# Decayed linear attention feeding a SwiGLU block: the second token tile enters by pairs of batches, and the last ramp evacuation moves to VectorE

## The chip, the cores and the metric

The kernel runs on one core of a Trainium2 chip. The metric is the device time of one execution in microseconds (us), the median of several runs. The engines are named as in the profile: PE is TensorE (matrix multiplication; PEld its weight loads), DVE is VectorE, ACT is ScalarE, POOL is GpSimd and SP is SyncE, which here only issues transfers.

## What is computed

Four batches, eight heads, 768 positions, 64 channels a head. Attention is linear with a decay per head, worked in blocks, with a state carried from block to block; its output, 3072 tokens by 512, goes through a SwiGLU block with 1536 inner features.

```python
for b in range(nb):                                   # blocks of positions
    intra = einsum('bhic,bhjc->bhij', qb, kb) * Dmask # lam**(i-j) below the diagonal
    intra = einsum('bhij,bhjd->bhid', intra, vb)
    inter = einsum('bhid,bhde->bhie', qb * lam_pow, kv_state)
    out[:, :, sl] = intra + inter
    kv_state = lam_block * kv_state + einsum('bhsd,bhse->bhde', kb * rev_pow, vb)
x = out.transpose(0, 2, 1, 3).reshape(B * S, H * D)
g = x @ w_gate
y = (g / (1 + exp(-g)) * (x @ w_val)) @ w_out
```

Inputs and output are float32; the kernel multiplies in bfloat16 and sums in float32.

## The kernel before

**Tiles.** The positions are cut into six tiles of 128 (`NBLK = 6`). A tile holds these 128 positions of all four batches, so 512 tokens. For each tile attention makes `xt`, the transposed input of the SwiGLU block (128 x 4 x 512, bfloat16), and the SwiGLU block then runs in 12 units, one for each 128 inner features, followed by output products for each batch.

**A unit** is `ffn_fc` (L404), made of `ffn_gv` and `ffn_h`: four matmuls of 512 columns into `gp` (L390), SiLU on ACT into `sil` (L392), four matmuls into `vp` (L395), and the product `h_sb` on DVE (L402). **An output** is `ffn_out` (L408): twelve matmuls over the inner features (L415), a copy `osb` on ACT (L418), and a transfer to memory on SP's queue (L419). Tile 0's outputs are made in two halves of 256 columns each, because `w_out` is loaded in two halves: the first half of columns after tile 0's units, the second half among tile 1's units.

**Attention pieces.** In tiles 0 and 1 the score matrix of a whole 128-position block is made. `prep_k` and `prep_q` (L227, L234) transpose k and q of one batch on PE, with the evacuation on ACT for k (L232) and on DVE for q (L238). `front0` (L263) makes the scores of a batch (L271) and DVE multiplies them by the decay mask into `ssb` (L275). `values0` (L280) multiplies by v (L291), in tile 1 also adds the state's part (L289), and `evac` (L277) brings the sum from PSUM to `xt` on ACT (L278). `scale_k` (L294) scales k on ACT for the state, one head at a time. `update0` (L309) multiplies the scaled k by v into `up` (L315) and decays the state in float32 on DVE (`kvd`, L321; in tile 1 first the sum, L319). `cast_kv` (L323) puts the state into bfloat16 on ACT (L326, L307).
From tile 2 on, a tile is handled in two halves of 64 positions, in two groups `p` of two batches: `turn` (L240) transposes k and q by a transfer on SP's queue; `scale_q` (L245, DVE L248) and `move_q` (L252, eight transfers on SP's queue) place the scaled q in `zbuf`; `front` (L356) makes the scores in the one buffer `spb` (L362); `masks` (L364) writes them to `zbuf` on DVE (L367, two instructions a group); `update` (L330) makes the state's sums (L338), `update_mid` (L341) the state in the middle of the tile on DVE (L343), `cast_mid` (L345) its copy in `ybuf` on ACT (L307, two a group); `values` (L369) multiplies (L377) and evacuates with `evac`.

**Order.** The program's order is written out by hand and is the order on each engine. A list of units is run through for each tile `tt` (L511 to L544), and after unit number i the attention pieces registered for i are run: `add(first, i, ...)` for those run during tile 0's units (they prepare tile 1), `add(second, i, ...)` for those during tile 1's (they finish tile 1's state and prepare tile 2). Each engine works strictly through its own list, waiting on semaphores.

**Ramp.** Before the first unit PE works through tile 0's attention (L422 to L444). `idle(n)` multiplies zeros n times, to keep PE at work while it waits; `values0(0, (b,), n)` does so n times ahead of the values of batch b, and `ffn_gv` twice ahead of the first unit.

**Loads.** POOL's queue takes them in this order after the ramp's: gate and value weights in seven slices of columns (`load_w`, L447), two clearings of `kvb` on POOL itself, q and k of tile 1 (whole tiles), the first half of `w_out` (`load_wo(0)`), v of tile 1 in two halves, k and q of tile 2. During tile 1 `hold(2)` (L259), a tiny copy on POOL that needs tile 2's transposed q, keeps the rest of POOL's queue back: the second half of `w_out`, tile 2's v, all of tile 3.

**PSUM.** Of eight banks, two are `spb` and six serve the pool `psum`, from which `gp`, `vp`, `up`, `op`, `tk`, `tq`, `sp` and `ffn_op` are taken.

Of the kernel before, what the change touches and what calls it, by code (L numbers as in the profile page):

```python
# [8 lines left out]
FP32 = mybir.dt.float32  # L9
BF16 = mybir.dt.bfloat16  # L10
U32 = mybir.dt.uint32
AF = mybir.ActivationFunctionType
ALU = mybir.AluOpType
# [8 lines left out]
def kernel(  # L22
# [16 lines left out]
    nc = tc.nc  # L39

    B, H, S, D = q.shape
    HP = H // 2
    BLK = 128
# [3 lines left out]
    MC = DM // 128  # L47
    FC = DFF // 128
    TT = B * BLK
# [9 lines left out]
    opool = ctx.enter_context(tc.tile_pool(name="opool", bufs=3))  # L59

    spsum = ctx.enter_context(tc.tile_pool(name="spsum", bufs=1, space=bass.MemoryType.PSUM))
    psum = ctx.enter_context(tc.tile_pool(name="psum", bufs=6, space=bass.MemoryType.PSUM))
# [21 lines left out]
    def load_nat(t, tt, b0=0, b1=B):  # L84

        d, name = (qn, "q_nat") if t is q else (kn, "k_nat") if t is k else (vn, "v_nat")
        if tt not in d:
            d[tt] = load.tile([128, B * H, D], BF16, name=name, tag=name)
        nc.gpsimd.dma_start(out=d[tt][:, b0 * H:b1 * H], in_=blk_ap(t, tt, b0, b1))  # L89
# [102 lines left out]
    wg_sb = const.tile([128, MC, DFF], BF16, name="wg_sb")  # L192
# [3 lines left out]
    def load_w(f0, f1):  # L196
        for t, w in ((wg_sb, moe_w_gate), (wv_sb, moe_w_val)):
            nc.gpsimd.dma_start(out=t[:, :, f0:f1], in_=w.rearrange("(c p) f -> p c f", p=128)[:, :, f0:f1])  # L198
# [15 lines left out]
    def xt_of(tt):  # L214
        if tt not in xts:
            xts[tt] = xpool.tile([128, MC, TT], BF16, name="xt", tag="xt")
        return xts[tt]
# [56 lines left out]
        for h in range(2):  # L274
            nc.vector.tensor_tensor(out=ssbs[tt, b][:, h], in0=sp[h], in1=mask0[:, h], op=ALU.mult)  # L275

    def evac(tt, b, op):  # L277
        nc.scalar.copy(out=xt_of(tt)[:, :, b * BLK:(b + 1) * BLK], in_=op)  # L278

    def values0(tt, bs, wait=0):  # L280

        for b in bs:
            op = psum.tile([128, HP, 128], FP32, name="op", tag="b")
            idle(wait, op.rearrange("p n t -> p (n t)"))
            ssb = ssbs.pop((tt, b))
            for hp in range(HP):
                i = b * HP + hp
                for h, ps in enumerate(HALVES if tt else ()):
                    nc.tensor.matmul(op[ps, hp, :], kvb[:, i, h, :], qts[tt][:, i, :], start=True, stop=False)  # L289
                for h, ps in enumerate(HALVES):  # L290
                    nc.tensor.matmul(op[ps, hp, :], vn[tt][:, 2 * i + h, :], ssb[:, h, hp, :], start=(tt == 0), stop=True)  # L291
            evac(tt, b, op)

    def scale_k(tt, h):  # L294

# [5 lines left out]
    def fp32_kv(name):  # L301
        return att.tile([128, NPP, D], FP32, name=name, tag=name)
# [6 lines left out]
    def update0(tt, p):  # L309

        up = psum.tile([128, NPP, D], FP32, name="up", tag="b")
        for n in range(NPP):
            for h, ps in enumerate(HALVES):
                i = 2 * (p * NPP + n) + h
                nc.tensor.matmul(up[ps, n, :], ks[tt][:, i, :], vn[tt][:, i, :], start=True, stop=True)  # L315
        kvn[p] = up
        if tt:
            kvn[p] = fp32_kv("kv32")
            nc.vector.tensor_tensor(out=kvn[p], in0=kvd[p], in1=up, op=ALU.add)  # L319
        kvd[p] = fp32_kv("kvd")  # L320
        nc.vector.tensor_tensor(out=kvd[p], in0=kvn[p], in1=lam64 if tt else lam128, op=ALU.mult)  # L321

# [58 lines left out]

    hs, gv = {}, {}

    def ffn_gv(tt, fc, wait=0):
        xt = xt_of(tt)
        fs = slice(fc * 128, (fc + 1) * 128)
        gp = psum.tile([128, TT], FP32, name="gp", tag="b")
        idle(wait, gp)
        for mc in range(MC):
            nc.tensor.matmul(gp, wg_sb[:, mc, fs], xt[:, mc, :], start=(mc == 0), stop=(mc == MC - 1))  # L390
        sil = opool.tile([128, TT], BF16, name="sil", tag="sil")
        nc.scalar.activation(sil, gp, AF.Silu)  # L392
        vp = psum.tile([128, TT], FP32, name="vp", tag="b")
        for mc in range(MC):
            nc.tensor.matmul(vp, wv_sb[:, mc, fs], xt[:, mc, :], start=(mc == 0), stop=(mc == MC - 1))  # L395
        gv[tt, fc] = sil, vp

    def ffn_h(tt, fc):
        sil, vp = gv.pop((tt, fc))
        if tt not in hs:  # L400
            hs[tt] = hpool.tile([128, FC, TT], BF16, name="h_sb", tag="h")
        nc.vector.tensor_tensor(out=hs[tt][:, fc, :], in0=sil, in1=vp, op=ALU.mult)  # L402

    def ffn_fc(tt, fc):  # L404
        ffn_gv(tt, fc, 2 if tt == fc == 0 else 0)
        ffn_h(tt, fc)

    def ffn_out(tt, b, i=0, parts=1):  # L408

# [31 lines left out]
    values0(0, (0,), 2)  # L441
    front0(0, 3)
    for b in range(1, B):
        values0(0, (b,), b)  # L444


    for f0, f1 in ((0, 128), (128, 256), (256, 512), (512, 768), (768, 1024), (1024, 1280), (1280, 1536)):  # L447
        load_w(f0, f1)
    for h, ps in enumerate(HALVES):
        nc.gpsimd.memset(kvb[ps, :, 1 - h].bitcast(U32), 0)  # L450
    load_nat(q, 1)
    load_nat(k, 1)
    load_wo(0)
    for b in (0, 2):
        load_nat(v, 1, b, b + 2)
    load_nat(k, 2)
    load_nat(q, 2)

# [1 line left out]
    def add(at, i, *piece):  # L460
        at.setdefault(i, []).append(piece)

    def attention(tt, at, sq, su, sf, sv):

        for p in range(2):
            add(at, sq[p], scale_q, tt, p)
            add(at, sq[p], move_q, tt, p)
            add(at, su[p], update, tt, p, range(1 if tt in (2, NBLK - 1) else 2))
        for p in range(2):
            add(at, sf[p], front, tt, p)  # L470
            add(at, su[p], update_mid, p)
            if 2 < tt < NBLK - 1:
                add(at, su[p], update_end, p)
                add(at, su[p] + 2, cast_kv, tt + 1, p)
            add(at, su[p] + 1, cast_mid, tt, p)
            add(at, sf[p], masks, tt, p)
        for b in range(B):
            add(at, sv, values, tt, b)

    first = {}  # L480
    for h in range(H):
        add(first, h // 2, scale_k, 0, h)
    for i in range(4):
        add(first, 5 + i, half_constants, i // 2, i % 2)
    for p in range(2):
        add(first, 4, update0, 0, p)
        add(first, 5 + p, cast_kv, 1, p)
    for b in range(B):
        add(first, 9 + b // 2, prep_q, 1, b)
        add(first, 11, prep_k, 1, b)  # L490
    for b in range(B):
        add(first, 11 + b // 2 + b // 3, front0, 1, b)
    for p in range(2):
        add(first, 14, values0, 1, range(2 * p, 2 * p + 2))
    add(first, 14, turn, 2, k)
    add(first, 14, turn, 2, q)
    second = {}
    add(second, 0, hold, 2)
    add(second, 0, load_wo, 1)
    add(second, 0, load_v, 2)  # L500
    add(second, 0, load_tile, 3)
    for h in range(H):
        add(second, h // 3, scale_k, 1, h)
    for h in range(H):
        add(second, (4, 4, 5, 5, 8, 8, 9, 9)[h], scale_k, 2, h)
    for p in range(2):
        add(second, 4, update0, 1, p)
        add(second, 6 + p, cast_kv, 2, p)
    attention(2, second, (5, 6), (11, 11), (6, 9), 14)

    for tt in range(NBLK):  # L511
        units = [(ffn_fc, tt, fc) for fc in range(FC)]
        if tt == 0:
            units += [(ffn_out, 0, b, 0, 2) for b in range(B)]
        elif tt == 1:
            outs = [(ffn_out, 0, b, 1, 2) for b in range(B)]
            units = units[0:10] + outs[0:1] + units[10:11] + outs[1:2] + units[11:12] + outs[2:4]
        else:
            units = sum([units[3 * b:3 * b + 3] + [(ffn_out, tt - 1, b)] for b in range(B)], [])
        pieces = {}  # L520
        if tt < 2:
            pieces = (first, second)[tt]
        elif tt + 1 < NBLK:
            for h in range(H):
                add(pieces, h // 2, scale_k, tt + 1, h)
            if tt == 2:
                for p in range(2):
                    add(pieces, 0, update, 2, p, (1,))
                for p in range(2):
                    add(pieces, p, update_end, p)  # L530
                    add(pieces, 4 + 4 * p, cast_kv, 3, p)
                attention(3, pieces, (3, 4), (5, 9), (5, 9), 13)
            else:
                attention(tt + 1, pieces, (1, 2), (4, 8), (4, 8), 12)
            if tt + 2 < NBLK:
                add(pieces, 4 if tt == 2 else 0, hold, tt + 1)
                add(pieces, 4 if tt == 2 else 0, load_tile, tt + 2)
        if tt and tt + 2 < NBLK:
            add(pieces, 14 if tt == 1 else 9, turn, tt + 2, k)
            add(pieces, 15 if tt == 1 else 10, turn, tt + 2, q)  # L540
        for i, (f, *at) in enumerate(units):
            f(*at)
            for g, *on in pieces.get(i, []):
                g(*on)  # L544
# [34 lines left out]
```

## Time and profile before

| | |
|---|---|
| median of 3 runs | 229.66 us (229.41, 229.66, 229.69) |
| the profiled execution's own time | 229.62 us |
| its span, first to last instruction | 227.8 us |
| granted PE clock, mean | 0.999 |
| first unit of tile 0 starts | 16.97 us |
| first unit of tile 1 starts | 50.59 us (first recorded matmul) |
| first unit of tile 2 starts | 80.94 us |
| DMA share in the first 53 us | nearly always 0.9 or more |

The span is counted from the first instruction to the last; the time of a run is some 1.8 us longer. All times of places in the trace below are from the span's start. In a row of the order of time the first number is the start, the second the busy length of the group, `x4` the number of instructions in it, and the bracket the idle time of the engine before it with what ended it. Lengths of single matmuls overlap, so the pace of PE is read from the start of one group to the start of the next. A few matmul records are missing, so a group may show `x3` where four ran; then the first recorded start is a little late.

### The profile page before, as it was taken

What the parts mean: (1) busy time and instruction counts of PE and PEld (TensorE: products, weight loads), DVE (VectorE), ACT (ScalarE), POOL (GpSimd) and SP (SyncE); (2) the same over time, 40 slices, a digit from 0 to 9 for tenths busy, and PEclk for the clock granted to TensorE, in tenths of its full rate; (3) what the DMA queues carried; (4) which work ended last, traced back from release to release, by engine and by line L of the source; (5) the groups of instructions that cost most, each with busy time, mean ns of one, the idle gap of its engine ahead of it and who ended that gap; (6) DMA issues with size and microseconds to landing.
All of it is one profiled execution on the core that took longest, in us unless ns stands there. A gap on an engine that the chain in (4) does not pass through costs nothing.

```text
span 227.8 us, 4780 instructions
## 1 busy us (share of the span) xinstructions
PE 219.6 (96%) x1958; PEld 111.4 (49%) x1984; DVE 111.6 (49%) x171; ACT 120.9 (53%) x232; POOL 50.6 (22%) x58
## 2 busy tenths in 40 slices
PE   7999999899999999999999999999999999999994
PEld 2544445584446754444544444544444544444443
DVE  2853575723697347769513977323853222232100
ACT  5857553458575765775755646565453532233222
POOL 7997915000581003700072000000000000000000
PEclk9999999999999999999999999999999999999999
DMA  7999999999599996999949979012211011011022
GB/s 111 150 170 195 196 169 179 165 180 182 92 160 197 171 173 160 164 183 170 178 66 161 212 165 122 21 49 71 68 49 46 3 46 46 0 49 47 39 99 92
DMA packets 108230, 27.32 MB, mean 120 GB/s; under 512 B 94256, under 2 KB 105776, under 8 KB 108208
## 3 DMA queue, kind: packets, MB, share of 16 engines
q0 software_dynamic: 82608, 13.90, 79.3%
q1 hardware_dynamic: 25456, 13.11, 25.5%
q8 instruction: 15, 0.25, 0.4%
q14 instruction: 7, 0.06, 0.1%
q10 hardware_dynamic: 144, 0.00, 0.0%
HBM read 28.32 MB, written 6.29 MB: 152 GB/s over the span
## 4 chain that ended last, share of the span: by engine, by line
PE 79%; DMA 10%; POOL 7%; issue 1%; DVE 1%; ACT 0%; ACTq 0%; POOLq 0%
PE ffn_op L415 28%; PE gp L390 23%; PE vp L395 22%; DMA wo_sb<-in_moe_w_out_dram 7%; DMA wv_sb<-in_moe_w_val_dram 3%; POOL k_nat L89 2%; PE op L377 2%; PE up L338 1%; POOL q_nat L89 1%; PE spb L362 1%; POOL v_nat L89 1%; POOL wv_sb L198 1%; POOL wg_sb L198 1%; POOL kvb L450 0%; PE op L289 0%
## 5 line engine op out<-in xcount | busy, mean ns | idle before, releaser
L402 DVE TENSOR_TENSOR h_sb<-sil,vp 128x512 bf16<-128x512 bf16 x72 | 49.0, 687 | 92.7 <-PE vp L395 76.2
L390 PE MATMUL gp<-xt,wg_sb 128*128 128x512 bf16 x269 | 72.4, 379 | 1.5 <-ACT xt L278 0.4
L395 PE MATMUL vp<-xt,wv_sb 128*128 128x512 bf16 x285 | 73.3, 379 | 0.1
L415 PE MATMUL ffn_op<-wo_sb,h_sb 128*128 128x512 bf16 (+1 forms) x346 | 66.2, 342 | 1.2 <-DMA wo_sb<-in_moe_w_out_dram 1.0
L392 ACT ACTIVATE sil<-gp 128x512 bf16<-128x512 f32 x72 | 43.1, 598 | 40.7 <-PE gp L390 39.0
L415 PEld LDWEIGHTS <-h_sb 128*128 128x128 bf16 x348 | 33.5, 98 | 30.1 <-DMA wo_sb<-in_moe_w_out_dram 1.2
L395 PEld LDWEIGHTS <-wv_sb 128*128 128x128 bf16 x288 | 28.2, 98 | 34.0
L418 ACT COPY osb<-ffn_op 128x512 f32<-128x512 f32 (+1 forms) x29 | 14.8, 511 | 54.7 <-PE ffn_op L415 54.6
L390 PEld LDWEIGHTS <-wg_sb 128*128 128x128 bf16 x288 | 27.0, 98 | 30.6 <-issue 0.6
L298 ACT ACTIVATE k_s<-k_nat,pw 128x256 bf16<-128x256 bf16 x48 | 21.4, 498 | 0.1
L367 DVE TENSOR_TENSOR zbuf<-spb,maskh 64x1024 bf16<-64x1024 f32 x16 | 19.5, 1218 | 0.1
L89 POOL DMA_DIRECT2D k_nat<-in_k_dram x9 | 12.1, 1351 | 7.5 <-PE vp L395 6.1
L261 POOL COPY held<-qt 128x2 bf16<-128x2 bf16 x3 | 1.0, 335 | 56.5 <-DMA qt<-q_nat 56.5
L278 ACT CAST xt<-op 128x512 bf16<-128x512 f32 x20 | 10.6, 592 | 4.4 <-PE op L291 2.7
L307 ACT CAST ybuf<-kv 64x512 bf16<-64x512 f32 x16 | 9.9, 616 | 0.3
L89 POOL DMA_DIRECT2D q_nat<-in_q_dram x6 | 9.7, 1609 | 1.6 <-DVE qt L238 1.6
L307 ACT CAST ybuf<-mid 64x512 bf16<-64x512 f32 x16 | 9.8, 616 | 0.2
L93 POOL DMA_DIRECT2D ybuf<-in_v_dram x8 | 8.8, 1110 | 2.4 <-issue 2.4
L209 PE MATMUL spb<-zeros 128*128 128x512 bf16 x20 | 7.3, 500 | 1.3 <-DVE warm L136 1.2
L275 DVE TENSOR_TENSOR ssb<-spb,mask 128x512 bf16<-128x512 f32 x8 | 5.2, 686 | 1.6 <-PE spb L271 1.6
L198 POOL DMA_DIRECT2D wv_sb<-in_moe_w_val_dram x7 | 5.4, 778 | 1.1 <-DMA wv_sb<-in_moe_w_val_dram 0.6
L198 POOL DMA_DIRECT2D wg_sb<-in_moe_w_gate_dram x7 | 5.5, 789 | 0.5 <-DMA wg_sb<-in_moe_w_gate_dram 0.5
(69 smaller groups left out, 124.8 us busy)
## 6 DMA issues: line engine op xcount, KB each, us to landing
out_dram<-osb SPq DMA_DIRECT2D x19, 256.0 KB, 2.0
q_nat<-in_q_dram POOLq DMA_DIRECT2D x5, 512.0 KB, 12.4
k_nat<-in_k_dram POOLq DMA_DIRECT2D x5, 512.0 KB, 13.7
ybuf<-in_v_dram POOLq DMA_DIRECT2D x8, 256.0 KB, 13.5
zbuf<-qs SPq DMA_DIRECT2D x32, 64.0 KB, 5.8
wo_sb<-in_moe_w_out_dram POOLq DMA_DIRECT2D x2, 768.0 KB, 12.1
wg_sb<-in_moe_w_gate_dram POOLq DMA_DIRECT2D x5, 256.0 KB, 8.9
wv_sb<-in_moe_w_val_dram POOLq DMA_DIRECT2D x5, 256.0 KB, 9.5
```

The source lines that it names most:

```text
L89: nc.gpsimd.dma_start(out=d[tt][:, b0 * H:b1 * H], in_=blk_ap(t, tt, b0, b1))
L198: nc.gpsimd.dma_start(out=t[:, :, f0:f1], in_=w.rearrange("(c p) f -> p c f", p=128)[:, :, f0:f1])
L278: nc.scalar.copy(out=xt_of(tt)[:, :, b * BLK:(b + 1) * BLK], in_=op)
L298: nc.scalar.activation(dst[:, :, h], kn[tt].rearrange("p (b h) d -> p b h d", b=B)[:, :, h], AF.Copy, scale=pw[:, h, e:e + 1])
L307: nc.scalar.copy(out=ybuf[HALVES[1 - c], tt % 2, c, p * NPP:(p + 1) * NPP, h], in_=t[HALVES[h]])
L367: nc.vector.tensor_tensor(out=zbuf[ps, :, c, n], in0=spb[ps], in1=maskh[ps], op=ALU.mult)
L390: nc.tensor.matmul(gp, wg_sb[:, mc, fs], xt[:, mc, :], start=(mc == 0), stop=(mc == MC - 1))
L392: nc.scalar.activation(sil, gp, AF.Silu)
L395: nc.tensor.matmul(vp, wv_sb[:, mc, fs], xt[:, mc, :], start=(mc == 0), stop=(mc == MC - 1))
L402: nc.vector.tensor_tensor(out=hs[tt][:, fc, :], in0=sil, in1=vp, op=ALU.mult)
L415: nc.tensor.matmul(op, hs[tt][:, fc, b * BLK:(b + 1) * BLK], wo_sb[:, fc, cs], start=(fc == 0), stop=(fc == FC - 1))
L418: nc.scalar.copy(out=osb, in_=op)
```

## The change

It has six parts.

1. `evac` and `values0` take an engine; in the ramp batch 3 of tile 0 is evacuated by DVE (`tensor_copy`), and in tile 1 batch 3 too. The numbers of zero multiplications ahead of tile 0's values change from 1, 2, 3 (batches 1 to 3) to 1, 1, 0, and ahead of the first unit from 2 to 3.
2. Tile 1's loads are split in pairs of batches: k and q of batches 0 and 1 come before the last 256 weight columns (now in two slices of 128), v of batches 0 and 1 after these, then the first half of `w_out`, then k, q, v of batches 2 and 3.
3. `update0` no longer decays the state; a new piece `decay0` does, at units 5 and 6 of tile 0's list, and at 9 and 10 of tile 1's.
4. Tile 1's attention pieces run by pairs: k, q, scores and values of batches 0 and 1 after units 7 to 11 of tile 0, those of batches 2 and 3 among the outputs behind.
5. The unit is split into `ffn_g` and `ffn_v` with a range of batches. Five units of tile 1 (`EARLY = 5`) run twice, in half width: for batches 0 and 1 in tile 0's list (four before the outputs, one after), for batches 2 and 3 at the head of tile 1's list.
6. In tile 1's list the four second-half outputs of tile 0 stand at the end, behind all units (before: among units 10 and 11). The transposing transfers of tile 2 move from behind tile 0's third output to behind the first half unit of tile 1's list, so behind all four outputs on SP's queue; `scale_k`, `update0`, `cast_kv`, `scale_q`, `front`, `masks` get later places.

```diff
-    def evac(tt, b, op):
-        nc.scalar.copy(out=xt_of(tt)[:, :, b * BLK:(b + 1) * BLK], in_=op)
-
-    def values0(tt, bs, wait=0):
+    def evac(tt, b, op, eng=None):
+        xt = xt_of(tt)[:, :, b * BLK:(b + 1) * BLK]
+        if eng is nc.vector:
+            nc.vector.tensor_copy(out=xt, in_=op)
+        else:
+            nc.scalar.copy(out=xt, in_=op)
+
+    def values0(tt, bs, wait=0, eng=None):
...
-            evac(tt, b, op)
+            evac(tt, b, op, eng)
...
             nc.vector.tensor_tensor(out=kvn[p], in0=kvd[p], in1=up, op=ALU.add)
+
+    def decay0(tt, p):
         kvd[p] = fp32_kv("kvd")
         nc.vector.tensor_tensor(out=kvd[p], in0=kvn[p], in1=lam64 if tt else lam128, op=ALU.mult)
...
-    def ffn_gv(tt, fc, wait=0):
-        xt = xt_of(tt)
+    def ffn_g(tt, fc, b0=0, b1=B, wait=0):
+
         fs = slice(fc * 128, (fc + 1) * 128)
-        gp = psum.tile([128, TT], FP32, name="gp", tag="b")
+        ts = slice(b0 * BLK, b1 * BLK)
+        gp = psum.tile([128, (b1 - b0) * BLK], FP32, name="gp", tag="b")
...
-    def ffn_fc(tt, fc):
-        ffn_gv(tt, fc, 2 if tt == fc == 0 else 0)
-        ffn_h(tt, fc)
+        nc.vector.tensor_tensor(out=hs[tt][:, fc, ts], in0=gv.pop((tt, fc)), in1=vp, op=ALU.mult)
+
+    def ffn_fc(tt, fc, b0=0, b1=B):
+        ffn_g(tt, fc, b0, b1, 3 if tt == fc == 0 else 0)
+        ffn_v(tt, fc, b0, b1)
...
-        values0(0, (b,), b)
+        values0(0, (b,), 1 if b < 3 else 0, nc.vector if b == 3 else None)
...
-    for f0, f1 in ((0, 128), (128, 256), (256, 512), (512, 768), (768, 1024), (1024, 1280), (1280, 1536)):
+    for f0, f1 in ((0, 128), (128, 256), (256, 512), (512, 768), (768, 1024), (1024, 1280)):
         load_w(f0, f1)
...
-    load_nat(q, 1)
-    load_nat(k, 1)
+    for t in (k, q):
+        load_nat(t, 1, 0, 2)
+    for f0, f1 in ((1280, 1408), (1408, 1536)):
+        load_w(f0, f1)
+    load_nat(v, 1, 0, 2)
     load_wo(0)
-    for b in (0, 2):
-        load_nat(v, 1, b, b + 2)
+    for t in (k, q, v):
+        load_nat(t, 1, 2, B)
     load_nat(k, 2)
     load_nat(q, 2)
...
+    EARLY = 5
...
-        add(first, 5 + i, half_constants, i // 2, i % 2)
+        add(first, 4 + i, half_constants, i // 2, i % 2)
     for p in range(2):
         add(first, 4, update0, 0, p)
+        add(first, 5 + p, decay0, 0, p)
         add(first, 5 + p, cast_kv, 1, p)
-    for b in range(B):
-        add(first, 9 + b // 2, prep_q, 1, b)
-        add(first, 11, prep_k, 1, b)
-    for b in range(B):
-        add(first, 11 + b // 2 + b // 3, front0, 1, b)
-    for p in range(2):
-        add(first, 14, values0, 1, range(2 * p, 2 * p + 2))
-    add(first, 14, turn, 2, k)
-    add(first, 14, turn, 2, q)
+
+    for b in range(2):
+        add(first, 7, prep_k, 1, b)
+        add(first, 8, prep_q, 1, b)
+        add(first, 9, front0, 1, b)
+        add(first, 10 + b, values0, 1, (b,))
+        add(first, 11 + EARLY, prep_k, 1, 2 + b)
+        add(first, 12 + EARLY, prep_q, 1, 2 + b)
+        add(first, 13 + EARLY, front0, 1, 2 + b)
+        add(first, 15 + EARLY, values0, 1, (2 + b,), 0, (None, nc.vector)[b])
     second = {}
+    add(second, 0, turn, 2, k)
+    add(second, 0, turn, 2, q)
     add(second, 0, hold, 2)
...
-        add(second, h // 3, scale_k, 1, h)
+        add(second, (0, 0, 1, 2, 3, 4, 5, 5)[h], scale_k, 1, h)
...
-        add(second, (4, 4, 5, 5, 8, 8, 9, 9)[h], scale_k, 2, h)
+        add(second, (6, 6, 7, 7, 8, 9, 10, 10)[h], scale_k, 2, h)
     for p in range(2):
-        add(second, 4, update0, 1, p)
-        add(second, 6 + p, cast_kv, 2, p)
-    attention(2, second, (5, 6), (11, 11), (6, 9), 14)
+        add(second, 6, update0, 1, p)
+        add(second, 9 + p, decay0, 1, p)
+        add(second, 8 + p, cast_kv, 2, p)
+    attention(2, second, (7, 8), (11, 11), (8, 10), 14)
...
         if tt == 0:
-            units += [(ffn_out, 0, b, 0, 2) for b in range(B)]
+            units[11:] = [(ffn_g, 0, 11), (ffn_v, 0, 11)]
+            units += [(ffn_fc, 1, fc, 0, 2) for fc in range(EARLY)]
+            units[-1:-1] = [(ffn_out, 0, b, 0, 2) for b in range(B)]
         elif tt == 1:
-            outs = [(ffn_out, 0, b, 1, 2) for b in range(B)]
-            units = units[0:10] + outs[0:1] + units[10:11] + outs[1:2] + units[11:12] + outs[2:4]
+            units[:EARLY] = [(ffn_fc, 1, fc, 2, B) for fc in range(EARLY)]
+            units += [(ffn_out, 0, b, 1, 2) for b in range(B)]
```

The arguments of `attention(tt, at, sq, su, sf, sv)` are the places of `scale_q` with `move_q`, of `update` with `update_mid` (and `cast_mid` one later), of `front` with `masks`, and of `values`.

More of the change, by code (lines that the diff above doesn't have):

```diff
@@ L382, with ffn_v @@
     hs, gv = {}, {}
-    def ffn_gv(tt, fc, wait=0):
-        xt = xt_of(tt)
+    def ffn_g(tt, fc, b0=0, b1=B, wait=0):
         fs = slice(fc * 128, (fc + 1) * 128)
-        gp = psum.tile([128, TT], FP32, name="gp", tag="b")
+        ts = slice(b0 * BLK, b1 * BLK)
+        gp = psum.tile([128, (b1 - b0) * BLK], FP32, name="gp", tag="b")
         idle(wait, gp)
         for mc in range(MC):
-            nc.tensor.matmul(gp, wg_sb[:, mc, fs], xt[:, mc, :], start=(mc == 0), stop=(mc == MC - 1))
-        sil = opool.tile([128, TT], BF16, name="sil", tag="sil")
+            nc.tensor.matmul(gp, wg_sb[:, mc, fs], xt_of(tt)[:, mc, ts], start=(mc == 0), stop=(mc == MC - 1))
+        sil = opool.tile([128, (b1 - b0) * BLK], BF16, name="sil", tag="sil")
         nc.scalar.activation(sil, gp, AF.Silu)
-        vp = psum.tile([128, TT], FP32, name="vp", tag="b")
+        gv[tt, fc] = sil
+    def ffn_v(tt, fc, b0=0, b1=B):
+        fs = slice(fc * 128, (fc + 1) * 128)
+        ts = slice(b0 * BLK, b1 * BLK)
+        vp = psum.tile([128, (b1 - b0) * BLK], FP32, name="vp", tag="b")
         for mc in range(MC):
[L395 to L399, printed above, removed]
+            nc.tensor.matmul(vp, wv_sb[:, mc, fs], xt_of(tt)[:, mc, ts], start=(mc == 0), stop=(mc == MC - 1))
         if tt not in hs:
             hs[tt] = hpool.tile([128, FC, TT], BF16, name="h_sb", tag="h")
-        nc.vector.tensor_tensor(out=hs[tt][:, fc, :], in0=sil, in1=vp, op=ALU.mult)
-    def ffn_fc(tt, fc):
-        ffn_gv(tt, fc, 2 if tt == fc == 0 else 0)
-        ffn_h(tt, fc)
+        nc.vector.tensor_tensor(out=hs[tt][:, fc, ts], in0=gv.pop((tt, fc)), in1=vp, op=ALU.mult)
+    def ffn_fc(tt, fc, b0=0, b1=B):
+        ffn_g(tt, fc, b0, b1, 3 if tt == fc == 0 else 0)
+        ffn_v(tt, fc, b0, b1)
     def ffn_out(tt, b, i=0, parts=1):
```

## The prediction

> **What bounds the kernel now.** I read the share of busy time first, then the waits of the matrix engine (PE), then the order of time at the three places the change touches. Engines first:
>
> ```profile
> PE 219.6 (96%) x1958; PEld 111.4 (49%) x1984; DVE 111.6 (49%) x171; ACT 120.9 (53%) x232; POOL 50.6 (22%) x58
> ```
>
> PE is busy 96% of 227.8 us and the granted clock is 0.999, so a gain must come from PE's few gaps. The waits that end on PE list them:
>
> ```profile
> PE ffn_op L415 <- DMA wo_sb<-in_moe_w_out_dram: 1.0, 1, 1.0
> PE spb L362 <- DVE qs L248: 0.5, 1, 0.5
> PE gp L390 <- ACT xt L278: 0.4, 1, 0.4
> ```
>
> Nothing else above 0.3 us is left but the 1.2 us at the very start, which is not touched. The ramp, in order of time (start, length):
>
> ```profile
> 14.78 0.41 PE L291 MATMUL op<-ssb,v_nat 128*64 128x128 bf16 x8
> 15.12 0.82 PE L209 MATMUL op<-zeros 128*128 128x512 bf16 x3
> 15.88 0.41 PE L291 MATMUL op<-ssb,v_nat 128*64 128x128 bf16 x8
> ...
> 16.33 0.58 ACT L278 CAST xt<-op 128x512 bf16<-128x512 f32 x1 [0.51 <-PE op L291]
> ...
> 16.97 1.02 PE L390 MATMUL gp<-xt,wg_sb 128*128 128x512 bf16 x4 [0.36 <-ACT xt L278]
> ```
>
> Three multiplications of zeros stand before batch 3's values, then ACT's evacuation, then the first unit at 16.97. The end of tile 1, ACT, DVE and PE:
>
> ```profile
> 65.15 2.45 DVE L367 TENSOR_TENSOR zbuf<-spb,maskh 64x1024 bf16<-64x1024 f32 x2
> 67.63 1.28 DVE L402 TENSOR_TENSOR h_sb<-sil,vp 128x512 bf16<-128x512 bf16 x2
> ...
> 70.53 2.45 DVE L367 TENSOR_TENSOR zbuf<-spb,maskh 64x1024 bf16<-64x1024 f32 x2
> ...
> 74.05 1.28 DVE L343 TENSOR_TENSOR mid<-kvd,up 128x512 f32<-128x512 f32 x2
> ...
> 75.68 2.54 ACT L307 CAST ybuf<-mid 64x512 bf16<-64x512 f32 x4
> ...
> 80.30 0.59 ACT L278 CAST xt<-spb 128x512 bf16<-128x512 f32 x1
> ...
> 80.94 1.02 PE L390 MATMUL gp<-xt,wg_sb 128*128 128x512 bf16 x3
> ```
>
> Mids on DVE, casts on ACT, values on PE, evacuations on ACT, and tile 2's first unit at 80.94: today that chain has its inputs early (update on PE at 73.27, mids at 74.05) and costs PE only 0.15 us (evacuation ends 80.89; PE would be free at 80.79).
>
> **The change, part by part.** One full unit takes PE 1.73 us (8 matmuls of 512 columns; starts at 52.32 and 54.05).
>
> *Ramp.* Four of the zero matmuls ahead of values go, one is added ahead of the first unit. Batch 2's values stay at 14.78 (its load lands at 14.73: issued 8.40, 6.3 us). Batch 3's follow at 15.12, not 15.88; its scores are ready (13.68 + 1.28 = 14.96). Its evacuation, now on DVE, starts at about 15.58. No such copy is in the trace: DVE reading 128x512 f32 from PSUM with one more operand takes 0.68 (L275, 0.64 from one to the next), a DVE cast from SBUF 0.71, ACT's cast 0.59. I take 0.66: end 16.24, first unit at 16.30, 0.67 earlier (0.6 to 0.75 by those ends). ACT's batch 2 cast ends at 15.81 and the three zero matmuls end near 16.2, so neither is later. But weights follow: the third chunk of wv (columns 256 to 511) was issued at 13.20 and took 7.40 us, landing at 20.60, and PE would now want it at 16.30 + 2 x 1.73 + 0.86 = 20.62. With its weight load that is a wait of about 0.1. Gain 0.55.
> The Trainium skill ("VectorE: DVE Perf Modes", Specifications) says that VectorE sits closer to SBUF and ScalarE closer to PSUM, which speaks against giving a PSUM evacuation to VectorE. The rows agree in size, 0.68 against 0.59; by that rule alone the move would cost 0.1, but it buys parallel work, since ACT would be free only at 15.81.
>
> *Loads on POOL's queue.* Tile 1's k and q for two batches come ahead of the last 256 weight columns, its v for two ahead of wo, the rest behind wo. Landings follow one another: 1.66 us for a 256 KB half (v: 44.07, 45.73), 0.72 for 128 weight columns, 1.33 for 256, 4.0 for wo. From 28.60 (the weights before them): k 30.3 to 30.9, q 32.5, four weight pieces to 35.4, v 37.1, wo 41.1, second k 42.8, q 44.4, v 46.1, then k and q of tile 2 near 49.7 and 53.3. PE's wants, with S = 16.42: k after eight units and the update, S + 14.6 = 31.0; q 33.0; v 37.9; weights of unit 10 at 36; wo 44.8. All are met, k narrowly (0 to 0.3 if not). So the wait of 1.02 for wo goes; in its place stands work of tile 1.
>
> *Five units split.* Twelve 256-column matmuls take 1.32 (77.10), so 0.110 each; ten half units cost 10 x 0.88 against 5 x 1.73: +0.15. The extra sil, h and k_s work (0.37 for a half evacuation against 0.59) lies beside PE: each half unit asks ACT for about 0.3 + 0.4 in 0.88.
>
> *Preparation in pairs.* Same matmuls: two batches of transposes 0.45 to 0.6, two of scores 0.7 to 0.9, four of values 1.91, and more changes between them and the units (about 0.1 each). Old sum 6.6, new 6.5 by the same rows; range -0.2 to +0.3, taken 0.0. Tile 1's first evacuations are hidden behind unit 11's second half and a half unit. One is not quite: the fourth osb needs the buffer of the first output, issued near 46.6; outputs took 6.2, 5.8, 5.9 us there, so 52.6, while the matmul ends at 51.6. ACT waits 1 us, and the pair's xt evacuation queued behind it ends at 53.6 where PE wants it at 53.5. +0.1 (0 to 0.4).
>
> *SP and what follows from it.* Tile 2's transposes now stand behind all four outputs: kt goes out at about 53.5 instead of 49.70, qt lands at about 61.4 instead of 59.08 (5.4 and 6.2 us without other loads, as at 133.54). POOL's held copy waits for it, and behind that wo's second half, tile 2's v, and tile 3's loads, all 2.3 later. v's first half would land at 71.7, just when the update wants it; wo at 69.9 is early. The wait for qs (0.52) goes: qs is wanted only at 65.
>
> *The end of tile 1.* The four outputs move behind all twelve units, masks and decays behind unit 8. By the program's order DVE then does: h8, qs, two masks, h9, decay, h10, decay, two masks, h11, two mids. One to the next from the rows above: 0.60, 0.60, 2.48, 0.62, 0.61, 0.62, 0.60, 2.48, 0.61, then 0.64 per mid: 9.86 to the first mid, 10.5 to the second, with no gap, since each input is ready before. From unit 8's end E (h starts 0.26 behind): mids at E + 10.1 and 10.8. Four casts (2.54) from 10.17, values of batches 0, 1 after two casts at 11.5, of 2, 3 after four at 12.8, two osb (0.26 each) and four xt evacuations (0.48 each) end at 15.15: tile 2 starts at E + 15.2. PE alone needs two fronts 0.92, three units 5.19, update 0.72, four outputs 5.28, values 1.13, changes 0.1: 13.34. So 1.87 us of wait where 0.15 was: +1.72. What it covers is late v (over 1 us of it).
>
> **Sum.** -0.55 - 1.02 - 0.52 + 0.15 + 0.1 + 1.72 = -0.12. The profiled execution's own time is 229.62 (span 227.8), 0.04 under the median of the three, so 229.5.
>
> **Rivals.** A difference under 0.2% (0.46 us) can't be told from none.
> *Gain kept.* If the tail is shorter than I chain it (PE's work fills it because casts and evacuations overlap more), up to 1.7 comes back: 227.8 at the best, 228.8 if half does. For: PE has few other gaps. Against: every link is a measured row and the order of DVE is fixed.
> *Transposes late in tile 2 (slower).* The pair of tile 3 took 9.8 us (79.42 to 89.21) with loads beside it until 84.96, the pair of tile 4 15.4 (99.22 to 114.58) beside loads all along, 8.0 at 133.54 with none. Now loads run to about 87.3: some 11.8 us, landing at 91.3. The front of tile 3 (93.26 before, about 93.2 now) needs qs 0.7 earlier, so it decides from 92.5 on. If the pair takes 15.4, it lands at 94.9 and costs 2.4: 231.9; halfway 230.6.
> *Clock falls in the thinned ramp (slower).* At the start the zero matmuls come every 0.43 us (weight loads at 1.60, 2.03, 2.46) and later every 0.22; one such stretch of 3.8 us would cost 1.9: 231.4. Against: PE idled 0.36 before 16.97 and did not slow.
> The Trainium skill ("TensorE: Matmul & The Clock Gate", Part 1) has the clock fall after an idle window of about 3.4 us; the new gaps are some 0.3, so by it there is no loss.
> *The change does not bite:* wo or k lands late and the old wait comes back, up to 1.0: 230.5.
>
> **Chances.** Forecast 0.45 (own range 229.0 to 230.1); gain kept 0.30; late transposes 0.14; clock 0.03; late loads 0.08. From these: faster 0.35 (gain kept and a part of the forecast's lower edge), same 0.37, slower 0.28. Range 228.4 to 230.6.
>
> **What would show it.** Right: first unit at 16.3; no wait of PE for wo; new waits of PE in values (L383) for ACT's casts and in tile 2's first gp for xt, about 1.9 us together; DVE without a gap from h8 to the mids; kt of tile 2 issued near 53.5. Wrong: those waits missing (then faster), the third wv chunk or k_nat holding PE for over 0.3, or PE waiting in tile 2's spb for qs (then slower).

## The result and the profile after

The changed kernel takes 231.24 us (median of 6 runs, 231.07 to 231.65) beside 229.55 us of the kernel before on the same chip (229.35 to 229.69). The ratio is 1.0078, 95% interval 1.0065 to 1.0091: slower by 0.8%, 1.7 us, and 0.6 us beyond the upper end of the range. The profiled execution has a span of 229.4 us where that of before had 227.8, at a granted clock of 1.0. In this profile the helpers stand on other lines: `gp` is L397, `vp` L407, `h_sb` L410, `sil` L399, the state's bfloat16 cast L332 (before L326), the decay L327 (L321), the first-half mids L349 (L343), values L383 (L377).

The engines' busy times on the page of after, and the waits that end on PE (total, how often, longest, in us):

```profile
PE 220.1 (96%) x1995; PEld 115.5 (50%) x2021; DVE 113.6 (50%) x178; ACT 121.0 (53%) x235; POOL 53.3 (23%) x62
```

```profile
PE vp L407 <- ACT kvb L332: 1.3, 1, 1.3
PE spb L209 <- DVE warm L136: 1.2, 1, 1.2
PE op L383 <- ACT ybuf L311: 0.8, 2, 0.4
PE gp L397 <- ACT xt L282: 0.4, 1, 0.4
PE gp L397 <- DVE h_sb L410: 0.3, 1, 0.3
```

PE's own work grew by 0.5 us (219.6 to 220.1) and the span by 1.5 (227.85 to 229.35), so most of the loss is waiting. The waits for `wo_sb` and `qs` are gone, as forecast. Those for `ybuf` and `xt` are the forecast ones of the end of tile 1. The first line and the last were not in the prediction. They lie in tile 0's units, between the state and unit 8 (the units of a tile are counted from 0). The order of time of after, first DVE, then ACT, then PE (start, length, and in the bracket the idle time before it with what ended it):

```profile
27.83 0.69 DVE L410 TENSOR_TENSOR h_sb<-sil,vp 128x512 bf16<-128x512 bf16 x1 [1.15 <-PE vp L407]
28.44 0.42 DVE L187 TENSOR_TENSOR maskh<-causal,pw 128x256 bf16<-128x256 bf16 x1
28.77 0.68 DVE L327 TENSOR_TENSOR kvd<-up,pw 128x512 f32<-128x512 f32 x1
31.32 0.69 DVE L410 TENSOR_TENSOR h_sb<-sil,vp 128x512 bf16<-128x512 bf16 x1 [1.86 <-ACT sil L399]
...
32.39 0.68 DVE L327 TENSOR_TENSOR kvd<-up,pw 128x512 f32<-128x512 f32 x1
...
29.49 1.17 ACT L332 CAST kvb<-up 64x512 bf16<-64x512 f32 x2 [1.99 <-DVE kvd L327]
30.69 0.60 ACT L399 ACTIVATE sil<-gp 128x512 bf16<-128x512 f32 x1
33.11 1.17 ACT L332 CAST kvb<-up 64x512 bf16<-64x512 f32 x2 [1.82 <-DVE kvd L327]
34.31 0.60 ACT L399 ACTIVATE sil<-gp 128x512 bf16<-128x512 f32 x1
...
31.02 0.70 PE L231 MATMUL tk<-identity,k_nat 128*128 128x128 bf16 x8
32.06 1.02 PE L397 MATMUL gp<-xt,wg_sb 128*128 128x512 bf16 x4 [0.34 <-DVE h_sb L410]
34.33 1.02 PE L407 MATMUL vp<-xt,wv_sb 128*128 128x512 bf16 x4 [1.25 <-ACT kvb L332]
```

Two engines hand the turn to each other. DVE's decay stands behind the unit's h and a constant; ACT's cast of the same `up` waits 1.99 us for that decay; the next unit's sil stands behind the cast on ACT; the next h on DVE waits 1.86 us for that sil; and the second decay stands behind this h, so that it all happens once more (1.82 us). PE runs ahead in the buffers that are free, until unit 8: its `gp` needs one that the late h holds, its `vp` the one of the second `up`, which the late cast holds. The kernel before had the same two readers of `up`, with the decays ahead of h:

```profile
26.48 1.28 DVE L321 TENSOR_TENSOR kvd<-up,pw 128x512 f32<-128x512 f32 x2
...
27.89 1.16 ACT L326 CAST kvb<-up 64x512 bf16<-64x512 f32 x2
...
29.68 1.16 ACT L326 CAST kvb<-up 64x512 bf16<-64x512 f32 x2
```

Both decays are done at 27.76, and neither cast has an idle bracket. The Trainium skill ("PSUM — Partial Sum Buffer", section "PSUM bank collisions raise a hardware error") says that the compiler's scheduler makes any two instructions of different engines on one bank and group of partitions follow one another, reads and reads too. By that rule a reader that moves makes the other reader late; the trace agrees, with 1.99 and 1.82 us. Which tool set the order in this program, no run shows.

The end of tile 1 in after, DVE, ACT and PE:

```profile
67.51 0.69 DVE L410 TENSOR_TENSOR h_sb<-sil,vp 128x512 bf16<-128x512 bf16 x1 [0.44 <-PE vp L407]
...
76.08 0.69 DVE L410 TENSOR_TENSOR h_sb<-sil,vp 128x512 bf16<-128x512 bf16 x1
76.69 1.27 DVE L349 TENSOR_TENSOR mid<-kvd,up 128x512 f32<-128x512 f32 x2
...
77.40 2.54 ACT L311 CAST ybuf<-mid 64x512 bf16<-64x512 f32 x4 [1.41 <-DVE mid L349]
...
78.13 0.25 PE L383 MATMUL op<-zbuf,ybuf 128*64 128x64 bf16 x3
78.71 0.86 PE L383 MATMUL op<-zbuf,ybuf 128*64 128x64 bf16 x32 [0.33 <-ACT ybuf L311]
80.00 0.41 PE L383 MATMUL op<-zbuf,ybuf 128*64 128x64 bf16 x13 [0.42 <-ACT ybuf L311]
...
82.45 1.02 PE L397 MATMUL gp<-xt,wg_sb 128*128 128x512 bf16 x3 [0.38 <-ACT xt L282]
```

Unit 8's matmuls end at 67.24 (h starts 0.27 behind), DVE has no gap from there to the mids, and tile 2 starts 15.2 us after 67.24: the number forecast. The brackets of PE's three waits add up to 1.13 us. By starts there is more: from the first values to tile 2's first unit it is 82.45 - 78.13 = 4.32 us, where the kernel before took 80.94 - 78.34 = 2.60:

```profile
78.34 0.95 PE L377 MATMUL op<-zbuf,ybuf 128*64 128x64 bf16 x48
...
80.94 1.02 PE L390 MATMUL gp<-xt,wg_sb 128*128 128x512 bf16 x3
```

### The profile page after: what moved, and what is told of

It is laid out like the page before. It is cut to its first block, busy times and chain, and to the rows that moved or that the text cites. A ratio compares the mean times of both kernels' runs of the same rounds, so it can differ in the third digit from the quotient of the medians.

```text
span 229.4 us, 4883 instructions
## 1 busy us (share of the span) xinstructions
PE 220.1 (96%) x1995; PEld 115.5 (50%) x2021; DVE 113.6 (50%) x178; ACT 121.0 (53%) x235; POOL 53.3 (23%) x62
## 4 chain that ended last, share of the span: by engine, by line
PE 85%; DVE 4%; issue 3%; DMA 3%; POOL 2%; ACT 2%; DVEq 0%; ACTq 0%; POOLq 0%
PE vp L407 26%; PE ffn_op L423 26%; PE gp L397 26%; DMA v_nat<-in_v_dram 3%; POOL k_nat L89 1%; PE op L383 1%; PE up L344 1%; PE spb L368 1%; DVE kvd L327 1%; PE op L295 1%; DVE h_sb L410 1%; ACT ybuf L311 1%; DVE zbuf L373 1%; PE op L293 1%; ACT kvb L332 1%
## 5 line engine op out<-in xcount | busy, mean ns | idle before, releaser
L410 DVE TENSOR_TENSOR h_sb<-sil,vp 128x512 bf16<-128x512 bf16 (+1 forms) x77 | 49.9, 652 | 87.1 <-PE vp L407 72.0
L407 PE MATMUL vp<-xt,wv_sb 128*128 128x512 bf16 (+1 forms) x302 | 73.8, 365 | 1.5 <-ACT kvb L332 1.3
L397 PE MATMUL gp<-xt,wg_sb 128*128 128x512 bf16 (+1 forms) x292 | 73.4, 365 | 1.8 <-ACT xt L282 0.4
L399 ACT ACTIVATE sil<-gp 128x512 bf16<-128x512 f32 (+1 forms) x77 | 44.0, 571 | 39.3 <-PE gp L397 37.3
L407 PEld LDWEIGHTS <-wv_sb 128*128 128x128 bf16 x308 | 30.1, 98 | 33.3 <-issue 1.7
L397 PEld LDWEIGHTS <-wg_sb 128*128 128x128 bf16 x308 | 28.6, 98 | 29.9 <-issue 1.6
L282 ACT CAST xt<-op 128x512 bf16<-128x512 f32 x18 | 9.7, 589 | 4.8 <-PE op L295 2.9
L248 DVE TENSOR_TENSOR qs<-qt,qsc 128x1024 bf16<-128x1024 bf16 x8 | 5.5, 685 | 2.7 <-DMA qt<-q_nat 2.7
L198 POOL DMA_DIRECT2D wv_sb<-in_moe_w_val_dram x8 | 6.2, 773 | 1.5 <-DMA wv_sb<-in_moe_w_val_dram 0.9
L198 POOL DMA_DIRECT2D wg_sb<-in_moe_w_gate_dram x8 | 6.3, 786 | 0.6 <-DMA wg_sb<-in_moe_w_gate_dram 0.6
```

What stands on the lines that cost most here:

```text
L282: nc.scalar.copy(out=xt, in_=op)
L397: nc.tensor.matmul(gp, wg_sb[:, mc, fs], xt_of(tt)[:, mc, ts], start=(mc == 0), stop=(mc == MC - 1))
L407: nc.tensor.matmul(vp, wv_sb[:, mc, fs], xt_of(tt)[:, mc, ts], start=(mc == 0), stop=(mc == MC - 1))
L410: nc.vector.tensor_tensor(out=hs[tt][:, fc, ts], in0=gv.pop((tt, fc)), in1=vp, op=ALU.mult)
```

## The experiments

Each ratio is to runs of the kernel before on the same chip in the same batch, whose medians were 229.58 to 229.63 us. "The first experiment's kernel" is the changed kernel with tile 0's decay put back.

**1. Is it the decay? Its place put back.**

```diff
-        add(first, 5 + p, decay0, 0, p)
+        add(first, 4, decay0, 0, p)
```

> The changed kernel with one line put back: tile 0's two decays stand at place 4, right behind the state, as before the change; everything else is as changed. Theory T1 (the decay): between units 5 and 8 of tile 0 ACT's cast of `up` waits for DVE's decay of the same buffer, DVE's decay waits behind h, and h waits for ACT's sil, which stands behind the cast; PE pays 1.25 + 0.34 us of it. Then with the decay at 4 both waits go: 231.24 - 1.6 = about 229.6 us, and the casts lie near 27.5 and 29 us instead of 29.49 and 33.11. Rival R1 (the buffers): the pair's preparation and the half constants take more PSUM banks between units 5 and 8 than before, and PE would wait there whatever DVE does: 231.2 us, a wait of some 1.3 us still at unit 7 or 8.

Measured 229.16 us, ratio 0.9982 (0.9972 to 0.9992): 2.1 us under the changed kernel by the medians, and faster than the kernel before. DVE, ACT and PE:

```profile
26.77 1.28 DVE L327 TENSOR_TENSOR kvd<-up,pw 128x512 f32<-128x512 f32 x2
...
27.56 1.16 ACT L332 CAST kvb<-up 64x512 bf16<-64x512 f32 x2
...
29.35 1.16 ACT L332 CAST kvb<-up 64x512 bf16<-64x512 f32 x2
...
31.18 0.61 PE L231 MATMUL tk<-identity,k_nat 128*128 128x128 bf16 x8
31.63 1.03 PE L397 MATMUL gp<-xt,wg_sb 128*128 128x512 bf16 x4
32.49 1.03 PE L407 MATMUL vp<-xt,wv_sb 128*128 128x512 bf16 x4
```

No wait is left at unit 8, with the same buffers and the same preparation: R1 falls. The gain is larger than the 1.6 us that the list of waits gave. By starts, from the transposes of k to unit 8's `vp` the changed kernel takes 34.33 - 31.02 = 3.31 us, this one 32.49 - 31.18 = 1.31: 2.0 us, of which the list shows 1.59.

**2. The decay late, but the cast ahead of it.**

```diff
-        add(first, 5 + p, decay0, 0, p)
         add(first, 5 + p, cast_kv, 1, p)
+        add(first, 5 + p, decay0, 0, p)
```

> The changed kernel with two lines exchanged: at places 5 and 6 of tile 0 the cast of `up` on ACT is listed ahead of the decay on DVE, which stays at 5 and 6. T1: the cast then waits for nothing, sil and h keep their pace, and the decay itself may be as late as it likes: about 229.6 us (1.6 less than the changed kernel), the casts near 27.5 and 29.2 us. If it is the decay's own place on DVE that costs (its 0.68 us ahead of the h that PE waits for) and not the cast behind it: only about 0.5 of it comes back, 230.7. R1: 231.2.

Measured 229.32 us, ratio 0.9991 (0.9981 to 1.0002). The first decay is as late as in the changed kernel (12.3 us after the first unit in both) and 1.9 us of the loss are gone, all but 0.2, which the intervals of these two experiments don't tell from none. So what cost was the cast's wait for the decay, not DVE's 0.68 us ahead of h:

```profile
27.71 1.16 ACT L332 CAST kvb<-up 64x512 bf16<-64x512 f32 x2
...
29.10 0.68 DVE L327 TENSOR_TENSOR kvd<-up,pw 128x512 f32<-128x512 f32 x1
29.88 0.69 DVE L410 TENSOR_TENSOR h_sb<-sil,vp 128x512 bf16<-128x512 bf16 x1
```

**3. The decay moved in the kernel before, nothing else.**

```diff
+    def decay0(tt, p):
         kvd[p] = fp32_kv("kvd")
...
+        add(first, 5 + p, decay0, 0, p)
         add(first, 5 + p, cast_kv, 1, p)
...
+        add(second, 4, decay0, 1, p)
```

> The kernel before with only tile 0's decays moved from place 4 to 5 and 6, ahead of the casts as in the change; tile 1's decays, the order of units, loads and ramp are as before. T1: the casts wait for the decays as in the changed kernel (waits of 1 to 2 us of ACT at the cast), and PE loses 0.3 to 1.6 us in tile 0: 229.9 to 231.1 us, the more of it the sooner PE wants the banks that hold `up`. Rival R1: no cost of its own, 229.55 us within 0.2.

Measured 229.91 us, ratio 1.0019 (1.0009 to 1.0029): a small loss, at the lower end of what was expected. The casts wait as in the changed kernel, and PE does too:

```profile
17.35 1.02 PE L392 MATMUL gp<-xt,wg_sb 128*128 128x512 bf16 x4 [0.36 <-ACT xt L278]
...
30.88 1.17 ACT L328 CAST kvb<-up 64x512 bf16<-64x512 f32 x2 [2.50 <-DVE kvd L323]
34.36 1.17 ACT L328 CAST kvb<-up 64x512 bf16<-64x512 f32 x2 [1.69 <-DVE kvd L323]
...
35.59 1.02 PE L397 MATMUL vp<-xt,wv_sb 128*128 128x512 bf16 x4 [0.73 <-ACT kvb L328]
...
42.71 1.48 PE L417 MATMUL ffn_op<-wo_sb,h_sb 128*128 128x256 bf16 x12
```

But PE's 1.02 us for `wo_sb` is missing in this profile: the first output, which waits for that load, comes 42.71 - 17.35 = 25.36 us after the first unit, where it was 42.45 - 16.97 = 25.48. What the ping-pong took, PE no longer had to wait for the load. The changed kernel had just removed that wait, and so paid in full. In these profiles the 0.3 us that is left isn't the ping-pong's: it lies ahead of the first unit (17.35, before 16.97), where the edit changes nothing, and from there to the end it is 210.8 us here and 210.9 before. Whether that holds for the other runs isn't shown.

**4. The ramp's part alone in the kernel before.**

```diff
-        ffn_gv(tt, fc, 2 if tt == fc == 0 else 0)
+        ffn_gv(tt, fc, 3 if tt == fc == 0 else 0)
...
-        values0(0, (b,), b)
+        values0(0, (b,), 1 if b < 3 else 0, nc.vector if b == 3 else None)
```

> The kernel before with the ramp's part alone: batch 3's values evacuated on VectorE, one multiplication of zeros ahead of batches 1 and 2, none ahead of 3, three ahead of the first unit. If the gain of the ramp is kept to the end: first unit near 16.45 instead of 16.97 us and the time 229.55 - 0.5 = 229.05 us. Rival: the gain is lost where tile 0 next waits for a transfer (wo at 43 us, qs of tile 1), since those come at a fixed time: PE's wait for wo grows from 1.0 to about 1.5 us and the time is 229.5.

Measured 229.64 us, ratio 1.0002 (0.9993 to 1.0011): nothing. The first unit does start at 16.34:

```profile
16.34 1.02 PE L394 MATMUL gp<-xt,wg_sb 128*128 128x512 bf16 x4
...
20.91 1.04 PE L399 MATMUL vp<-xt,wv_sb 128*128 128x512 bf16 x4
...
34.94 0.62 PE L237 MATMUL tq<-identity,q_nat 128*128 128x128 bf16 x8 [0.18 <-DMA q_nat<-in_q_dram]
```

`vp` at 20.91 stands 1.12 us behind its `gp` (19.79) instead of 0.86: the third chunk of wv landed at 20.86. Then tile 1's q, whole, landed at 34.90, and at 42.2 `wo_sb` with the same 1.02 us of wait. The rival held, though the wait for `wo_sb` didn't grow as it said: the time was lost earlier.

**5. The ramp's part undone in the first experiment's kernel**, where the pair's loads come early.

```diff
-        ffn_g(tt, fc, b0, b1, 3 if tt == fc == 0 else 0)
+        ffn_g(tt, fc, b0, b1, 2 if tt == fc == 0 else 0)
...
-        values0(0, (b,), 1 if b < 3 else 0, nc.vector if b == 3 else None)
+        values0(0, (b,), b)
```

> The first experiment's kernel with the ramp as before the change (1, 2 and 3 multiplications of zeros, 2 ahead of the first unit, batch 3's values evacuated on ScalarE). In the old order of loads the ramp's part alone gained nothing (229.64 against 229.60): PE ran into the third chunk of wv and into tile 1's q. Theory: with the pair's loads early the 0.5 us are kept, so without them 229.16 + 0.5 = about 229.65 us. Rival: they are lost here too, to a landing that PE meets: 229.2.

Measured 229.69 us, ratio 1.0007 (0.9998 to 1.0016), 0.53 us above the first experiment. In the profile the first unit starts at 17.05 (there 16.64), and tile 2's first unit 63.86 us later in both, so nothing of the difference is lost on the way. The profiled run was the longest of its ten (230.21 us); it also has a wait of 0.45 us for `qs` in tile 2. The same edit is worth nothing in one order of loads and half a microsecond in the other.

**6. The end of tile 1**, in the first experiment's kernel: the outputs among the units again, the attention a place earlier, and both.

```diff
-            units += [(ffn_out, 0, b, 1, 2) for b in range(B)]
+            outs = [(ffn_out, 0, b, 1, 2) for b in range(B)]
+            units[10:] = [outs[0], units[10], outs[1], units[11], *outs[2:]]
```

> The first experiment's kernel (tile 0's decay at place 4) with tile 1's four outputs again between its last units, as before the change: output, unit 10, output, unit 11, output, output. Theory T2: in the changed order VectorE's chain from h8 to the mids sets the start of tile 2, and PE's waits of 0.34 + 0.42 in the values and 0.38 ahead of tile 2's first unit (some 0.5 us more in starts) are its price. With unit 11 behind the update, h11 (0.61 us) comes after the mids, so everything behind them is 0.6 us earlier: 229.16 - 0.6 = about 228.6 us. Rival: the waits are ScalarE's (its two outputs' evacuations and eight casts and copies in a row) and stay: 229.2.

```diff
-    attention(2, second, (7, 8), (11, 11), (8, 10), 14)
+    attention(2, second, (6, 7), (11, 11), (7, 9), 14)
```

> The first experiment's kernel with tile 2's attention one place earlier in tile 1: qs and its moves at places 6 and 7, fronts and masks at 7 and 9 (not 7, 8 and 8, 10); the outputs stay behind the units. T2: VectorE idles 0.57 + 0.44 us between the state and the first masks (61.97 to 66.75 in the trace of the first experiment), and the masks then fill it: mids 1.0 us earlier, tile 2 starts 1.0 us earlier: about 228.2 us. Rival: tile 2's queries have not come by then (they land at 59.5) or ScalarE's chain sets the end: 229.2.

> Both edits of the tail in the first experiment's kernel. T2: the two gains add, 0.6 + 1.0 = 1.6 us of the 1.87 us that tile 2's start lost, so PE waits there for 0.3 us at most and the time is about 227.6 us, the fastest of all. If another chain takes over (ScalarE's casts, or the moves of q on SP landing after PE wants them), between 228.0 and 228.6.

Measured: outputs among the units 228.92 us, ratio 0.9979 (0.9964 to 0.9993); attention earlier 229.47, 0.9994 (0.9980 to 1.0007); both 228.88, 0.9976 (0.9961 to 0.9991). The expected 0.6, 1.0 and 1.6 us came out as 0.2, a loss of 0.3, and 0.3, and the runs of each spread over 1.5 to 1.7 us, where the first experiment's spread over 0.45; by the intervals of the ratios none of the three is told apart from the first experiment. T2's mechanism is in the trace all the same: with the attention earlier, from the first unit (16.97) to tile 2's first unit (79.84) it is 62.87 us, in the first experiment (16.64 to 80.50) 63.86, the 1.0 us expected. With the outputs among the units alone it is 63.58, 0.3 of the 0.6 expected, since PE waits 0.56 us for the second half of `w_out` there (landed 68.06). What was won is lost to transfers. PE's waits with both edits (in a run of 229.59 us, 0.7 above the median), and with the attention alone earlier PE and DVE in tile 2:

```profile
PE spb L368 <- DVE qs L248: 1.0, 2, 0.9
PE ffn_op L423 <- DMA wo_sb<-in_moe_w_out_dram: 0.7, 1, 0.7
```

```profile
92.88 0.31 PE L368 MATMUL spb<-qs,kt 64*64 64x64 bf16 x14 [0.55 <-DVE qs L248]
...
92.13 0.69 DVE L248 TENSOR_TENSOR qs<-qt,qsc 128x1024 bf16<-128x1024 bf16 x1 [3.77 <-DMA qt<-q_nat]
```

Tile 2 now starts early enough that tile 3's transposes are late for it, and an output among the units wants the second half of `w_out` before it has landed (69.04 with both edits).

**7. The transposes earlier on SP's queue**, after both edits of the tail and after the second alone.

```diff
+    add(first, 18, turn, 2, k)
+    add(first, 18, turn, 2, q)
...
-    add(second, 0, turn, 2, k)
-    add(second, 0, turn, 2, q)
...
-            add(pieces, 15 if tt == 1 else 10, turn, tt + 2, q)
+            add(pieces, 14 if tt == 1 else 10, turn, tt + 2, q)
```

> The kernel with both edits of the tail, and only SP's order changed: tile 2's two transposes stand behind the second of tile 0's outputs instead of behind all four, and tile 3's second transpose stands ahead of the last output of tile 1, not behind it. Theory T3: what ate the tail's gain are transfers behind the transposes: in the trace of both edits PE waits 0.67 us for wo's second half (landed 69.04) and 0.85 us in tile 2 for qs behind tile 3's second transpose (landed 92.47). With k of tile 2 at 49.4 and q at 53.2 us the transposes are issued 3 and 2 us earlier and land near 58.7 instead of 60.16, all that POOL's held copy releases comes 1.4 us earlier, and both waits shrink to 0.2 us or less: 228.88 - 1.2 = about 227.7 us, and less scatter. Rival: the pair lands with the q load whatever its place (the load sets it), so wo and tile 3's loads come no earlier: 228.7 to 228.9.

> The same order of SP in the kernel whose attention alone is earlier (the four outputs stay behind all units). Here wo's second half is wanted only at 72.7 us, so one of the two waits is missing; PE's 0.55 us for qs in tile 2 goes and the 0.38 us ahead of tile 2's first unit stays: T3 gives 229.47 - 0.7 = about 228.7 us, 1.0 us above the other kernel of this pair. Rival: no change, 229.5.

Measured 228.20 us, ratio 0.9950 (0.9934 to 0.9966), and 228.27 us, ratio 0.9954 (0.9937 to 0.9972): both beat the kernel before by 0.5% and the changed kernel by 3.0 us. Against the same kernels without this edit that is 0.7 us less with both edits of the tail (the intervals overlap a little) and 1.2 less with the second alone (clear of noise). T3 is right in its mechanism; the two didn't differ by the 1.0 us that was expected of them, and one run of six in each still took some 1.1 us more than the rest (229.26, 229.32). Order of time of the first of them, DVE to the mids, then PE:

```profile
64.71 2.45 DVE L373 TENSOR_TENSOR zbuf<-spb,maskh 64x1024 bf16<-64x1024 f32 x2
...
72.95 1.28 DVE L349 TENSOR_TENSOR mid<-kvd,up 128x512 f32<-128x512 f32 x2
...
67.90 1.48 PE L423 MATMUL ffn_op<-wo_sb,h_sb 128*128 128x256 bf16 x12
...
78.93 1.02 PE L397 MATMUL gp<-xt,wg_sb 128*128 128x512 bf16 x4 [0.20 <-ACT xt L282]
...
91.63 0.44 PE L368 MATMUL spb<-qs,kt 64*64 64x64 bf16 x32 [0.21 <-DVE qs L248]
```

The output at 67.90 no longer waits (`w_out` landed at 67.19), tile 2 starts 1.57 us earlier than in the first experiment (0.31 of it from a ramp that began earlier in this profile), and the wait in tile 2 is 0.21 where it was 0.85 in the longer run profiled with both edits. In the second of them tile 2's first unit comes 62.86 us after tile 0's, a full 1.0 us less than in the first experiment, and the scores made in tile 2 (91.82) no longer wait.

## Why the prediction was wrong

**The step that failed.** "The change, part by part" has no term for part 3 in tile 0. The text before the prediction says that `decay0` comes at units 5 and 6 of tile 0's list; the sum costs tile 1's decays in DVE's chain, and tile 0's it leaves at nothing without a word. What had hidden the cast's dependence on the decay was the decay's place directly behind the state: both done at 27.76, the first cast at 27.89. With that cover gone the cost is 2.0 us by starts; experiment 1 removes it by the decay's place and experiment 2 by the cast's. None of the rivals had it. What was to be asked of a piece that moves is who else reads its input, and what is queued behind that reader.

**The sum without it** was nearly right. The forecast was 229.5 and the first experiment, the change less this one move, took 229.16. Term by term:

- *Ramp, -0.55.* Right in size: 0.53 by experiment 5, of which the first units in the profiles show 0.41 (17.05 against 16.64). In the changed kernel's profile the first unit started at 16.48, not 16.30, since v of batches 0 and 1 landed 0.31 later there (13.05) and held the first values by 0.18. DVE's evacuation took 0.69 us (taken at 0.66). The Trainium skill ("VectorE: DVE Perf Modes", Specifications) puts VectorE closer to SBUF and ScalarE closer to PSUM; the trace agrees in direction, 0.69 against ACT's 0.59 us, and the rule changed nothing, as said. The 0.1 for the third chunk of wv was not due in the changed kernel, where PE came at 20.79 and the chunk had landed at 20.57; with a first unit at 16.34 (experiment 4) it was 0.26.
- *`wo_sb` -1.02 and `qs` -0.52.* Both waits are gone.
- *Five split units, +0.15.* The pace of a half unit is 0.88 (42.95 to 43.83), as taken.
- *Preparation in pairs 0.0, fourth osb +0.1.* Together too dear. From the first unit to tile 2's first it was 63.97 us before; less 1.02 and 0.52, plus 0.15 and 1.72, that is 64.30, and the first experiment took 63.86. These two terms are therefore -0.44 by subtraction and not +0.1. The fourth osb cost nothing: in the changed kernel the first output landed at 53.02, ahead of the copy at 53.48; in the first experiment the copy at 52.01 did follow the landing at 51.91, but PE's next unit stood right behind the values (52.39). Read from start to start, with the gaps ahead of them, the pieces of the preparation took 5.59 us before and 5.37 in the first experiment, the lower end of what was taken for them (-0.2), and tile 0's four outputs, which the sum leaves alone, 5.57 and 5.43. That is -0.36 of the -0.44.
- *The end of tile 1, +1.72.* Right: 15.2 us after unit 8, by the chain that was written down, and 4.32 - 2.60 = 1.72 by starts. The waits forecast at about 1.9 together show 1.13 in their brackets, less than the starts do, as at unit 8.

In the two profiles the change is -0.49 us ahead of the first unit, +2.00 from there to tile 2's first unit (65.97 against 63.97), and -0.01 behind it: 1.50 of span, where the medians differ by 1.69. The +2.00 is 2.11 for the decay (65.97 against the first experiment's 63.86) and -0.11 for all the other terms.

**The rivals.** *Gain kept* was wrong for the changed kernel and wrong in its reason (the tail is as long as chained), but the tail can be shortened, as experiments 6 and 7 show. *Late transposes* did not strike the changed kernel: tile 3's qt landed at 93.20, past the 92.5 that was given, but tile 2 itself was 1.5 us late and wanted its scores only at 94.77. In the first experiment, without the loss, qt landed at 91.08 and PE didn't wait either. In the fifth, with the same tail, it landed at 93.08 and PE waited 0.45 us; with a shorter tail it was 0.55 and 0.85. So the rival's wait is there, but smaller than its 2.4, and it comes and goes with the landing. *Clock*: granted 1.0, no fall. *Late loads*: all were met.

## What to carry to other kernels

When a piece of work is moved away from its producer, list the other readers of the same buffer and the instructions behind those readers; a cast that had been free can start to hand the turn back and forth between two engines. A wait that PE has is also a cover for others: an edit costed in a kernel with such a wait (experiments 3 and 4) shows less, cost and gain alike, than after the wait has gone. And after a stall is shortened, look at the transfers behind it first, since they keep their own times.

## What the runs showed of the hardware

Putting tile 2's first transpose 3.5 us earlier on SP (52.95 to 49.42) made the second land only 1.5 us earlier (60.16 to 58.62): the first held SP's queue until 53.51, and the second's input landed at 53.70 (both edits of the tail, without and with experiment 7's). Beside loads the transpose of tile 3's k remained slow, 77.42 to 89.32, where that of tile 5's k, with loads beside it only until 133.62, took 131.89 to 137.43. The landing of tile 3's q differed from profile to profile (89.93 to 92.47 in experiments 6 and 7), which is a likely reason, not a tested one, for the spread of 1.5 us in experiment 6.
